# Delta-rule attention woven into a feed-forward layer: inverses by halves for every block, one block at a time, and Gram products on quarters of the array

## The chip, the core and the metric

The kernel runs on one core of one Trainium2 chip. The core's engines each run their own instructions in order: PE (TensorE, matmuls; PEld are its weight loads), DVE (VectorE), ACT (ScalarE), POOL (GpSimd) and SP (SyncE, which here only issues transfers). The metric is the device time of one execution in microseconds (us); the time shown for a kernel is the median of its runs. A profile is one execution recorded by the hardware profiler.

## The reference

Four sequences of 768 tokens, eight heads of 48 columns. First a recurrence over the tokens of each (sequence, head), then a feed-forward layer on what it gives, all in float32:

```python
k_n = k / (np.linalg.norm(k, axis=-1, keepdims=True) + 1e-06)
for t in range(S):                       # S = 768, state is 48 x 48 per (sequence, head)
    kt, vt, bt = (k_n[:, :, t], v[:, :, t], beta[:, :, t, None])
    y[:, :, t] = np.einsum('bhd,bhde->bhe', q[:, :, t], state)
    v_old = np.einsum('bhde,bhd->bhe', state, kt)
    state = state + bt[:, :, :, None] * np.einsum('bhd,bhe->bhde', kt, vt - v_old)

x = y.transpose(0, 2, 1, 3).reshape(B * S, H * D)       # 3072 x 384
h = x @ w_in                                            # w_in 384 x 2048
out = np.maximum(0.01 * h, h) @ w_out                   # w_out 2048 x 384
```

The two weight arrays arrive as float64.

## The kernel before

**Blocks.** The tokens are cut into chunks of 64. A block is the next chunk of all four sequences, so 256 tokens and 32 (sequence, head) pairs, in two groups of two sequences; there are twelve blocks. With G = K K^T of a chunk, n the norms and c = beta / n^2, a chunk needs T = (I + strict_lower(diag(c) G))^-1 diag(c) and A = strict_lower(Q K^T); then W = T n V - Kt S with Kt = T K, the next state S' = S + K^T W, and y = Q S + A W.

**Streams.** Five generators produce the work, each a few instructions per step:

- `weights`: 32 halves of weight rows. Each is converted from float64 words to an exact sum of two float32r parts: five or six DVE instructions of 384 columns (clamp L155, then L172, L173, L175, L176, or L160 to L166 for the nine in `FORMB`), ACT's absolute value and cast, POOL's sum and difference.
- `gram` (blocks in turn): for each sequence ACT writes K^T into a block-diagonal operand `kd` (`diag`, L109, two copies of 0.5 us), four matmuls of 96 rows, 128 by 128, give [G | A^T] of four pairs of heads in one PSUM tile (L279), ACT copies it to `gs` (L285), and a product with a triangle masks A^T (L286, on POOL; DVE in block 0 as L283 and block 1). G goes to DRAM (`gd`), A^T too (`ad`), and both are read back in other layouts: `gd` to the elimination's L and, for the blocks by halves, to `gm`; `ad` to the lower rows of the operand ring `rq`.
- `inv` (batches of blocks): T^T by elimination of columns on DVE. `eliminate` does for each column a product into `tmp` (L359 or L361) and a subtraction from T (L364), each often in two instructions for the even and odd rows. Blocks 0 and 1, each alone, and the pairs 2, 3 and 4, 5 go by halves: the two diagonal halves of 32 rows of each chunk are inverted on partitions of their own (31 columns), and the full T^T is put together later. The pairs 6, 7 and 8, 9 and 10, 11 go whole (`inv_whole`, 63 columns, 128 partitions). The results go to DRAM (`td`).
- `solve` (blocks in turn): loads the rings `rt` (T^T), `rv`, `rk`, `rq`; for blocks by halves `merge` multiplies the halves together on PE (`pz` L488, `pu` L496, with copies `zs` L490 on ACT and DVE between). Then `kt` (`pk` L558, and POOL's n V at L563), `step_w` (`pw` L571), `step_s` (`pc` L579), `step_y` (`py` L587), each 32 matmuls of a block and alternating between the two column halves of the array, and six transfers of y^T into `xl`, which is x^T of the block.
- `ffn` (blocks in turn): `xl` is split into `xh` and the rest (three pieces, ACT and DVE). For each of 16 slices f of the hidden layer nine matmuls of 256 columns give `ph` (L644); the relu is ACT's 0.01 h (L650) and DVE's maximum `t` (L651); ACT casts it to `gh` (L115), POOL takes the difference `gl` (L116); six matmuls of 384 columns add into `po` (L635), two slices later (`PD` = 2). `ph` has two buffers. At the end ACT copies `po` to `ob` (L666) and it is written.

**Order.** `weave` emits these streams side by side, at even paces set by a table of numbers at the end of the file; a scheduler then orders the instructions of each engine. Each engine runs its own list in order, so an instruction that waits holds up all behind it. `mark` and `behind` put some transfers behind a named instruction.

Of the kernel before, what the change touches and what calls it, by code (L numbers as in the profile page):

```python
# [30 lines left out]
HC = C // 2  # L31
P = 128
NCST = C + 64 + HS + 2 + 2
# [6 lines left out]
KQ_BUFS = 3  # L40
KT_BUFS, Q_BUFS = 2, 2
# [9 lines left out]
def delta_moe_kernel(ctx: ExitStack, tc, kqT, kv, qT, beta, cst, w_all, out, nblk):  # L51
    """A block holds the next chunk of each of the sequences.

    Recurrence of a chunk with G = K K^T, n = |k| + eps, c = beta / n^2:
      T = (I + strict_lower(diag(c) G))^-1 diag(c),  Kt = T K,  A = strict_lower(Q K^T)
      W = T n V - Kt S,  S' = S + K^T W,  y = Q S + A W
    """
# [7 lines left out]
    dr = ctx.enter_context(tc.tile_pool(name="dr", bufs=3, space=DRAM))  # L65
# [4 lines left out]
    NB = batches(nblk)  # L70
    where = {n: (b, i) for b, ns in enumerate(NB) for i, n in enumerate(ns)}
    Lh, gm = {}, {}

# [4 lines left out]
    eye0 = csb[:, C + 64:C + 64 + HS]    # of row (block, half, inverse), to column (inverse)  # L78
    blk = csb[0:HD, C + 64 + HS:C + 66 + HS]     # column h: row is of head h
    half = csb[:, C + 66 + HS:]  # L80
# [6 lines left out]

    def statics():
        for t in ring["t"]:
            nc.vector.memset(t, 0.0)  # L90
        for x in "vq":
            for t in ring[x]:
                nc.gpsimd.memset(t[0:R0], 0.0)

    def identities():
        with behind("rec"):
            for t in ring["k"]:
                nc.vector.tensor_copy(
                    t[0:R0].rearrange("p h u t -> p (h u) t"),
                    eye[:, 0:D].rearrange("p (o t) -> p o t", o=1).broadcast_to([R0, GH, D]))  # L100

    def dq(act):
        """The queue that a transfer is issued on"""
        return (nc.sync, nc.scalar)[act]

    def diag(dst, src, cols):
        """[row, pair, x] to [row, pair, h, x], 0 where the row is not of head h"""
        for h in range(2):
            nc.scalar.mul(dst[:, :, h], src, cols[:, h:h + 1])  # L109

# [1 line left out]
    wi, wo = ([{}, {}] for _ in range(2))  # L112
# [4 lines left out]

    def weights():
        """From float64 words to float32 (round to nearest; below float32's range to 0, above it to
        its largest), then to the two parts: sign, exponent and 20 bits of the fraction are taken  # L120
        from the high word, the low word counts 2^-52 of the exponent's power of two."""
        raws = {}

        def load(k):
            if k < 2 * NFC:
                raws[k] = raw = sb.tile([P, DO], U64, tag=f"w{k}", name=f"wr{k}", bufs=1)
                if k >= WAHEAD:     # not before the work on an earlier part, which this waits for
                    with behind("norms" if WGATE <= k < WGATE + 2 else "work"):
                        nc.vector.memset(raw[:, 0:1].bitcast(F32), 0.0)
                nc.sync.dma_start(raw, w_all[:, k // 2, k % 2])  # L130

        with behind("kq"):
            for k in range(WAHEAD):
                load(k)
        for k in range(2 * NFC):
# [5 lines left out]
            r = sb.tile([P, DO], F32, tag="cr", name=f"cr{k}", bufs=CB)  # L141
# [12 lines left out]
            with behind("rec" if RECA <= k < RECB else None):  # L154
                i = nc.vector.tensor_scalar(g, g, HI_MIN, HI_MAX, ALU.max, ALU.min)  # L155
            mark["work"] = i.ins
            load(k + WAHEAD)
            if k in FORMB:
                # the first part is cut off after 11 bits of the fraction, the second has the 23 bits behind them
# [11 lines left out]
            else:  # L171
                nc.vector.tensor_scalar(gi, gi, 3, 0x3FFFFFF8, ALU.logical_shift_left, ALU.bitwise_and)  # L172
                nc.vector.scalar_tensor_tensor(gi, hii, 0xC0000000, gi, ALU.bitwise_and, ALU.bitwise_or)  # L173
                if k in FORMD:
                    nc.vector.tensor_scalar(ri, gi, 0xFF800000, None, ALU.bitwise_and)  # L175
                    nc.vector.scalar_tensor_tensor(r, loi, 2.0 ** -52, r, ALU.mult, ALU.mult)  # L176
                else:
                    nc.scalar.mul(r, loi, 2.0 ** -52)
                    e = place("we", F32, DO)
                    nc.vector.tensor_scalar(e.bitcast(U32), gi, 0xFF800000, None, ALU.bitwise_and)  # L180
                    nc.gpsimd.tensor_tensor(r, r, e, ALU.mult)
# [5 lines left out]
    Gdr, Adr, Tdr, nrm, xls, mark = {}, {}, {}, {}, {}, {}  # L187

    def behind(name):
        """What is traced here is issued behind the marked instruction, on its engine."""  # L190
        return tc.issue_after(mark[name]) if name in mark else nullcontext()

    Lw, done = {}, set()

    def need(gen, fn, *blocks):
        for n in blocks:
            while (fn, n) not in done:
                next(gen)

    def by_halves(b):  # L200
        return b < NH

    def rows_of(b, i, e, g=None):
        """Partitions of a block's halves of inverses, (half, group, h, unit)"""
        a, w = i * 64 + e * HS, HS
        if g is not None:
            a, w = a + g * GH, GH
        return slice(a, a + w)

    def odd(b):  # L210
        """Whether a batch has the odd rows of T^T on partitions of their own, behind the even ones"""
        return by_halves(b) and len(NB[b]) == 1

# [26 lines left out]
    def gram(n):  # L240
# [9 lines left out]
        def load():  # L250
            if not ahead:
                return
# [555 lines left out]
```

## Time and profile before

| | us |
|---|---|
| median of 3 runs (lowest, highest) | 802.52 (793.92, 803.21) |
| span of the profiled execution | 800.6 |
| first FFN matmul | 113.5 |
| end of FFN block 0 (its copies of `ob`) | 202.65 |
| ends of blocks 1 to 5 | 269.76, 343.95, 411.40, 474.55, 530.83 |
| ends of blocks 6 to 11 | 568.36, 632.45, 673.28, 728.82, 762.78, 794.83 |

Two lines of the page's list of groups show how such a line is read: line of the code, engine, operation, output and input by the program's names, shape, count; then busy time and mean ns of one; then idle time of the engine just before them and what ended it.

```profile
L361 DVE SCALAR_TENSOR_TENSOR tmp<-T,cb,LA 128x252 f32<-128x252 f32 (+44 forms) x186 | 87.5, 503 | 2.2 <-POOL T L400 2.1
L109 ACT ACTIVATE kd<-kq,csb 96x256 f32<-96x256 f32 x94 | 42.1, 500 | 11.6 <-DMA kq<-in_kqT 10.9
```

A window's line has its start and end and its length, then for PE, PEld, DVE, ACT and POOL the busy time with the number of instructions, then the clock granted to PE as a share of full speed, the share of DMA time and GB/s. In a timeline a line is a start, a duration, the engine and the instruction with the count of equal neighbours; what stands in brackets is the idle time before it and what ended it. A matmul on float32 shows as two records. Times of matmuls are modelled at their ends, so a busy PE is not PE at its peak.

### The profile page before, as it was taken

Reading aid. Unit: us, or ns where it says so; the run is one execution under the profiler, and the core shown is the slowest. Engines: PE = TensorE matmul, PEld = TensorE weight load, DVE = VectorE, ACT = ScalarE, POOL = GpSimd, SP = SyncE. Lnnn points to the kernel's source line nnn. Section 1 sums busy time; section 2 is a strip of 40 time slices with the busy share of each in tenths; the row PEclk is TensorE's granted clock in tenths of the full one; section 3 lists DMA queues with packets and bytes.
Section 4 is the critical chain, followed back from the end, with each engine's and each line's share of the span. In section 5 each row is a group of like instructions: output and inputs, shape, how many; then the busy total and the mean of one; then the engine's idle time right before and its main releaser. Section 6 shows DMA issues by size and latency. Waiting matters only on the chain.

```text
span 800.6 us, 18926 instructions
## 1 busy us (share of the span) xinstructions
PE 648.8 (81%) x7000; PEld 600.8 (75%) x7000; DVE 602.9 (75%) x1684; ACT 380.1 (47%) x903; POOL 338.5 (42%) x371
## 2 busy tenths in 40 slices
PE   3343627786989897996998989989897999899997
PEld 3242516675989786986987978879786888899997
DVE  6988999999759308999994799996899997012221
ACT  5535543476547554553564353433634323545342
POOL 4327566755534433335336234344244343133332
PEclk9999957997997999897899999999999999999999
DMA  7987547532764596475325552312433102321000
GB/s 232 228 206 165 159 118 175 102 93 68 173 126 120 113 226 156 103 162 133 76 70 142 113 127 54 87 40 56 101 80 87 41 1 49 99 66 40 1 22 20
DMA packets 147547, 84.65 MB, mean 106 GB/s; under 512 B 114432, under 2 KB 126848, under 8 KB 147072
## 3 DMA queue, kind: packets, MB, share of 16 engines
q1 hardware_dynamic: 143120, 82.97, 43.8%
q8 instruction: 55, 0.90, 0.5%
q10 hardware_dynamic: 4336, 0.48, 0.5%
q14 instruction: 36, 0.29, 0.1%
HBM read 55.89 MB, written 22.81 MB: 98 GB/s over the span
## 4 chain that ended last, share of the span: by engine, by line
DVE 47%; PE 26%; DMA 14%; issue 5%; SPq 3%; ACT 2%; POOL 1%; DVEq 0%; ACTq 0%; POOLq 0%
DVE tmp L361 14%; DVE T L364 14%; PE ph L644 10%; PE po L635 10%; DVE t L651 4%; DVE tmp L359 3%; DMA td<-T 2%; PE pg L279 2%; DMA LA<-gd 2%; PE pk L558 2%; DMA rt<-td 2%; DVE cg L173 1%; DMA wr<-in_w_all 1%; DMA rq<-in_qT 1%; DVE cg L155 1%
## 5 line engine op out<-in xcount | busy, mean ns | idle before, releaser
L116 POOL TENSOR_TENSOR gl<-t,gh 128x256 fp32r<-128x256 f32 x192 | 163.9, 855 | 332.1 <-ACT gh L115 262.0
L644 PE MATMUL ph<-xh,w 128*128 128x256 f32 x1152 | 256.9, 300 | 42.4 <-DVE t L651 30.1
L644 PEld LDWEIGHTS ph<-xh,w 128*128 128x128 f32 x1152 | 200.7, 200 | 56.3 <-DVE t L651 40.4
L364 DVE TENSOR_TENSOR T<-T,tmp 128x120 f32<-128x120 f32 (+53 forms) x555 | 191.5, 375 | 0.9
L635 PE MATMUL po<-w,gh 128*128 128x384 f32 x768 | 187.4, 351 | 2.8 <-ACT gh L115 2.8
L115 ACT CAST gh<-t 128x256 fp32r<-128x256 f32 x192 | 77.6, 406 | 226.0 <-DVE t L651 191.1
L651 DVE TENSOR_TENSOR t<-ph,t 128x256 f32<-128x256 f32 x192 | 80.0, 418 | 136.1 <-ACT t L650 135.4
L644 PE MATMUL ph<-xl,w 128*128 128x256 f32 x576 | 169.2, 295 | 5.7 <-DVE xl L116 5.7
L635 PEld LDWEIGHTS po<-w,gh 128*128 128x128 f32 x768 | 135.2, 198 | 5.0 <-ACT gh L115 4.1
L644 PEld LDWEIGHTS ph<-xl,w 128*128 128x128 f32 x576 | 115.0, 200 | 7.7 <-DVE xl L116 7.2
L635 PE MATMUL po<-w,gl 128*128 128x384 f32 x384 | 116.2, 354 | 1.7 <-POOL gl L116 1.5
L650 ACT ACTIVATE t<-ph 128x256 f32<-128x256 f32 x192 | 72.5, 382 | 81.2 <-PE ph L644 69.5
L279 PE MATMUL pg<-kq,kd 96*128 96x128 f32 x376 | 68.0, 343 | 31.2 <-ACT kd L109 28.1
L361 DVE SCALAR_TENSOR_TENSOR tmp<-T,cb,LA 128x252 f32<-128x252 f32 (+44 forms) x186 | 87.5, 503 | 2.2 <-POOL T L400 2.1
L361 DVE SCALAR_TENSOR_TENSOR tmp<-T,cb,LB 128x220 f32<-128x220 f32 (+43 forms) x186 | 88.5, 504 | 0.1
L279 PEld LDWEIGHTS pg<-kq,kd 96*128 96x128 f32 x376 | 61.3, 247 | 35.2 <-ACT kd L109 30.5
L635 PEld LDWEIGHTS po<-w,gl 128*128 128x128 f32 x384 | 71.1, 196 | 4.7 <-POOL gl L116 3.6
L359 DVE TENSOR_TENSOR tmp<-T,Lh 128x28 f32<-128x28 f32 (+42 forms) x183 | 59.2, 347 | 0.7
L286 POOL TENSOR_TENSOR gs<-gs,csb 128x256 f32<-128x256 f32 x40 | 35.9, 901 | 33.9 <-ACT gs L285 28.6
L563 POOL TENSOR_TENSOR rv<-rv,nt 64x384 f32<-64x384 f32 x48 | 43.4, 934 | 15.1 <-issue 13.4
L109 ACT ACTIVATE kd<-kq,csb 96x256 f32<-96x256 f32 x94 | 42.1, 500 | 11.6 <-DMA kq<-in_kqT 10.9
L183 POOL TENSOR_TENSOR cg<-cg,cr 128x384 f32<-128x384 f32 x23 | 27.9, 1218 | 30.9 <-DVE cr L176 30.9
(89 smaller groups left out, 718.9 us busy)
## 6 DMA issues: line engine op xcount, KB each, us to landing
wr<-in_w_all SPq DMA_DIRECT2D x32, 384.0 KB, 4.0
kq<-in_kqT SPq DMA_DIRECT2D x47, 192.0 KB, 3.8
gd<-gs SPq DMA_DIRECT2D x48, 128.0 KB, 3.1
ad<-gs SPq DMA_DIRECT2D x24, 256.0 KB, 3.2
rq<-ad SPq DMA_DIRECT2D x24, 256.0 KB, 4.8
rv<-in_kv SPq DMA_DIRECT2D x24, 192.0 KB, 4.6
rk<-in_kv SPq DMA_DIRECT2D x24, 192.0 KB, 4.0
rq<-in_qT SPq DMA_DIRECT2D x24, 192.0 KB, 4.2
```

Of the source, the lines that this page charges most:

```text
L109: nc.scalar.mul(dst[:, :, h], src, cols[:, h:h + 1])
L115: nc.scalar.copy(hi, src)
L116: lo_eng.tensor_tensor(lo, src, hi.bitcast(F32), ALU.subtract)
L279: nc.tensor.matmul(pv[:, :, p], kd[:, p].rearrange("p h t -> p (h t)"), kq[:, p], start=True, stop=True)
L359: nc.vector.tensor_tensor(tv, a, l, ALU.mult)
L361: nc.vector.scalar_tensor_tensor(tv, a, c[:, j:j + 1], l, ALU.mult, ALU.mult)
L364: i = nc.vector.tensor_tensor(t, t, tv, ALU.subtract)
L563: nc.gpsimd.tensor_tensor(v[DN, :, us], v[DN, :, us], nt[DN, g, :, us].rearrange("p h (u o) -> p h u o", o=1).broadcast_to([C, 2, NPAIR, D ...
L635: nc.tensor.matmul(po[t][:, :DO], a[:, ts_], w[f], start=(f == 0 and k == 0), stop=(f == NFC - 1 and k == 2))
L644: nc.tensor.matmul(ph[:, :TB], a[f][:, cc * P:(cc + 1) * P], x[:, cc], start=(k == 0), stop=(k == 3 * NCC - 1))
L650: nc.scalar.mul(t, ph[:, :TB], 0.01)
L651: nc.vector.tensor_tensor(t, ph[:, :TB], t, ALU.max)
```

## The change

- Every block's inverse goes by halves, one block at a time: 16 rows on 128 partitions, 31 columns, even and odd rows in two instructions each (60 products at L269 and 60 subtractions at L274 per block). `inv_whole` is gone, `merge` runs for all blocks (`pz` L325, `pu` L333).
- Gram: `kd` is gone. K^T and Q^T of the two parities of heads lie on partitions 0 to 47 and 64 to 111; 32 matmuls of a block (L202, 48 rows, 64 by 128) each take a quarter of the array: row half b, column half c, head c ^ b. Two PSUM tiles per group.
- The results go straight into operands: A^T is masked on DVE from PSUM into the ring `rq` (L217, four of 64x256 per group), the lower left of G is copied by POOL into `gm` (L221). Only the diagonal halves of G go through DRAM, in eight transfers (L210), and come back contiguous (L226). `ad` and the read of `gm` from DRAM are gone. The inverse goes to DRAM as `td` (L299) and `tt` (L301).
- The queue of those transfers is ACT's for blocks 0 and 1, SP's for the others (`dq`).
- The order is written out: FFN of block n with `solve` of n + 1, the inverse of n + 2, `gram` of n + 3. Weights: eight beside the first inverse, eight beside the second, the rest beside the first FFN block; `rq` has four buffers instead of two, `cr` two instead of three.

```diff
-def batches(nblk):
-    return [[0], [1]] + [[n, n + 1] for n in range(2, nblk, 2)]
+    def dq(n):
+        return nc.scalar if n < 2 else nc.sync
...
     def gram(n):
-            kd = sb.tile([P, NPAIR, 2, C], F32, tag="yt", name=f"kd{n}_{q}", bufs=YT_BUFS)[0:HD]
-            diag(kd, kq[:, :, 0], blk)
             for p in range(NPAIR):
-                nc.tensor.matmul(pv[:, :, p], kd[:, p].rearrange("p h t -> p (h t)"), kq[:, p], start=True, stop=True)
-                nc.scalar.copy(gs[:, :, us], pv)
-                (nc.vector if n == 0 else nc.gpsimd).tensor_tensor(gs[:, 1, us], gs[:, 1, us], trib, ALU.mult)
-                        nc.sync.dma_start(gd[g, h].rearrange("u j i -> j u i"), gs[h * C:(h + 1) * C, 0])
-                    nc.sync.dma_start(ad[g], gs[:, 1])
+                for c in range(2):
+                    for b in range(2):
+                        r = slice(b * R0, b * R0 + D)
+                        nc.tensor.matmul(ps[b][c * 64:(c + 1) * 64, p * 128:(p + 1) * 128],
+                                         kq[r, c ^ b, p, 0], kq[r, c ^ b, p].rearrange("p x t -> p (x t)"),
+                                         start=True, stop=True)
+            for b in range(2):
+                nc.scalar.copy(gs[:, b], pv[b][:, 0])
+                    dq(n).dma_start(
+                        gd[a:a + GU].rearrange("l j i -> j l i"),
+                        gs[c * 64 + e * HC:c * 64 + (e + 1) * HC].rearrange("p b u t -> p (b u) t")[:, :, e * HC:(e + 1) * HC])
+                    nc.vector.tensor_tensor(
+                        qa[DN, c, b * NPAIR:(b + 1) * NPAIR], pv[b][r, 1],
+                        tri[r].rearrange("p (o t) -> p o t", o=1).broadcast_to([C, NPAIR, C]), ALU.mult)
+                nc.gpsimd.tensor_copy(m[R0 + HC:P, c].rearrange("p (b u) t -> p b u t", b=2),
+                                      gs[c * 64 + HC:(c + 1) * 64, :, :, 0:HC])
...
     def inv(n):
+        for j in range(HC - 1):
+            eliminate(n, L, j, T, j // 2 + 1)
+                nc.vector.tensor_copy(Tt.rearrange("p i m -> p m i"), T)
+                        dq(n).dma_start(td[e].rearrange("(m x) l i -> x l m i", x=2)[er], T[a:a + HS])
+                    dq(n).dma_start(tt.rearrange("l i (x m) -> x l i m", x=2)[er], Tt[er * 64:er * 64 + HS])
...
     def merge(n, g, t):
-            nc.sync.dma_start(t[R0 + e * HC:R0 + (e + 1) * HC].rearrange("p h u i -> p (h u) i")[:, :, e * HC:(e + 1) * HC],
-                              td[0, :, rows_of(b, i, e, g)])
+            dq(n).dma_start(t[R0 + e * HC:R0 + (e + 1) * HC].rearrange("p h u i -> p (h u) i")[:, :, e * HC:(e + 1) * HC],
+                            T[e, :, gl])
+        dq(n).dma_start(gt[0:HC], Tt[gl].rearrange("l i m -> i l m"))
...
-    weave(nblk * NF,
-          (gg, G2, 0, GB), (gg, G, GB, LEADG),
-          (iv, inv_steps(2), IV0, I2), (iv, sum(inv_steps(b) for b in range(3, len(NB))), I2, I2 + (nblk - 4) * LEADI),
-          (sv, m * NS, 0, m * LEADS),
-          (wg, 2 * NFC, 0, WE), (chain(ffn, range(nblk)), nblk * NF, 0, nblk * NF))
+    weave(32, (iv, NI, 0, 32), (gg, NGR, 0, 8), (wg, W0, 0, 32))
+    identities()
+    weave(32, (sv, NS, 0, 24), (iv, NI, 0, 32), (wg, W1, 0, 32), (gg, NGR, 26, 32))
+    for n in range(nblk):
+        weave(NF, (ff, NF, 0, NF), (wg, 2 * NFC, 0, 12),
+              (sv, NS if n + 1 < nblk else 0, 0, 12), (iv, NI if n + 2 < nblk else 0, 0, NF), (gg, NGR if n + 3 < nblk else 0, 8, NF))
...
-WG, WS, WE, W0, W1, RECA, RECB = 5, 0, 12, 6, 6, 0, 32
+W0, W1 = 8, 8
```

What the scheduler made of it shows in each engine's list. First DVE, where the first split of x (`xl`, the last thing before the first FFN matmul can go) stands. Before, ahead of it are 20 clamps (L155), and it lies amid the columns of the second inverse and a weight:

```order
L155 TENSOR_SCALAR cg_1323<-cg_1323 128x384
L129 MEMSET wr_1327 128x2
L364 TENSOR_TENSOR T_787<-T_787,tmp_19_0_975 128x2x5x12
L172 TENSOR_SCALAR cg_1323<-cg_1323 128x384
L359 TENSOR_TENSOR tmp_20_0_994<-T_787,Lh_210 128x132
L116 TENSOR_TENSOR xl_696<-xl_696,xh_1289 128x256
L173 SCALAR_TENSOR_TENSOR cg_1323<-wr_1071,cg_1323 128x384
L364 TENSOR_TENSOR T_787<-T_787,tmp_20_0_994 128x2x6x11
L116 TENSOR_TENSOR xl_696<-xl_696,xh_1289 128x256
```

After, ahead of it are all 32 clamps (now L144), the whole second inverse and the masks of the next gram:

```order
L269 TENSOR_TENSOR tmp_30_0_1183<-T_607,L_323 128x8
L274 TENSOR_TENSOR T_607<-T_607,tmp_30_0_1183 128x8
L293 COPY Tt_608<-T_607 128x16x32
L217 TENSOR_TENSOR rq_75<-pg_0_0_1135,csb 64x256 x2
L217 TENSOR_TENSOR rq_75<-pg_0_1_1136,csb 64x256 x2
L217 TENSOR_TENSOR rq_76<-pg_1_0_1215,csb 64x256 x2
L111 TENSOR_TENSOR xl_658<-xl_658,xh_1248 128x256
L217 TENSOR_TENSOR rq_76<-pg_1_1_1216,csb 64x256 x2
L111 TENSOR_TENSOR xl_658<-xl_658,xh_1248 128x256 x2
```

So the twelve weights that stood behind the first split of x now stand ahead of it, as does the end of the second inverse.

Second, ACT at the same place. Before, the casts of x are followed by the first activation at once:

```order
L519 COPY nt_1399<-pn_1397 64x32
L115 CAST xh_1289<-xl_696 128x256
L115 CAST w_1270<-cg_1259 128x384
L115 CAST xh_1289<-xl_696 128x256
L115 CAST w_1285<-cg_1274 128x384
L115 CAST xh_1289<-xl_696 128x256
L650 ACTIVATE t_0_1308<-ph_0_1298 128x256
```

After, the transfers of the second inverse (`td`, `tt` out, `rt`, `gm` in) are issued between, on the same engine:

```order
L206 COPY gs_1_1213<-pg_1_1_1216 128x256
L110 CAST xh_1248<-xl_658 128x256 x2
L350 COPY nt_1465<-pn_1463 64x32
L312 DMA rt_79<-td_1190 32x16x32 x2
L314 DMA gm_0_218<-tt_1191 32x16x32
L312 DMA rt_80<-td_1190 32x16x32 x2
L320 COPY gm_0_218<-gm_0_218 32x16x2x16
L314 DMA gm_1_292<-tt_1191 32x16x32
L465 ACTIVATE t_0_1267<-ph_0_1257 128x256
```

The first activation of FFN block 0 now stands behind a read of `td`, which waits for its write, and behind a copy of what was read.

Third, PE in the FFN. Before, a gram of one sequence is four matmuls in a row, between the products of the FFN:

```order
L496 MATMUL pu_1_3310<-zs_1_3291,gm_1_3285 32x32 x16
L279 MATMUL pg_1_3366<-kq_1_3205,kd_1_3367 128x128 x4
L279 MATMUL pg_2_3380<-kq_2_3207,kd_2_3381 128x128 x4
L644 MATMUL ph_2_3651<-xh_3542,w_254 128x256
```

After, a group is sixteen matmuls whose PSUM tiles alternate; the second group of a block is cut up by `ph` and `po`:

```order
L451 MATMUL po_1_1256<-w_1621,gl_12_2180 128x384
L202 MATMUL pg_1_0_2390<-kq_1_2206 64x128
L202 MATMUL pg_1_1_2391<-kq_1_2206 64x128
L202 MATMUL pg_1_0_2390<-kq_1_2206 64x128
L202 MATMUL pg_1_1_2391<-kq_1_2206 64x128
L460 MATMUL ph_15_2312<-xh_1248,w_1760 128x256
```

The number of places behind the first `ph` where PE's list goes from products of the FFN to others or back is 181 before and 291 after.

More of the change, by code (lines that the diff above doesn't have):

```diff
@@ L32 @@
 P = 128
[L33 removed]
+NCST = C + 64 + HS + 2
 EPS = 1e-6
@@ L95, in identities, with behind @@
     def identities():
[L96 to L109, printed above, removed]
+        for t in ring["k"]:
+            nc.vector.tensor_copy(
+                t[0:R0].rearrange("p h u t -> p (h u) t"),
+                eye[:, 0:D].rearrange("p (o t) -> p o t", o=1).broadcast_to([R0, GH, D]))
     wi, wo = ([{}, {}] for _ in range(2))
+    raws, mark = {}, {}
+    def behind(name):
+        return tc.issue_after(mark[name]) if name in mark else nullcontext()
     def split(src, hi, lo, lo_eng):
@@ L116, in split, with load_w @@
         lo_eng.tensor_tensor(lo, src, hi.bitcast(F32), ALU.subtract)
-    def weights():
[L122 to L134, printed above, removed]
+    def load_w(k):
+        if k < 2 * NFC:
+            raws[k] = raw = sb.tile([P, DO], U64, tag=f"w{k}", name=f"wr{k}", bufs=1)
+            if "work" in mark:
+                with behind("work"):
+                    nc.vector.memset(raw[:, 0:1].bitcast(F32), 0.0)
+            nc.sync.dma_start(raw, w_all[:, k // 2, k % 2])
+    def weights():
         for k in range(2 * NFC):
@@ L185, in weights @@
             yield
[L187 to L208, printed above, removed]
@@ L457, in inv_halves @@
+                Tts[n] = td, tt
+                done.add((inv, n))
             yield
[L459 to L463 removed]
     def merge(n, g, t):
[L467 to L477 removed]
+        T, Tt = Tts[n]
```

492 lines of the change are left out of this document (150 added, 342 removed).

## The prediction

> **What bounds the kernel now.** I read the page's busy shares first, then its 40 slices, then windows cut at the first FFN product and at the copies of `ob` that end each FFN block, then the waits of PE.
>
> ```profile
> PE 648.8 (81%) x7000; PEld 600.8 (75%) x7000; DVE 602.9 (75%) x1684; ACT 380.1 (47%) x903; POOL 338.5 (42%) x371
> ...
> PE   3343627786989897996998989989897999899997
> ...
> DVE  6988999999759308999994799996899997012221
> ```
>
> ```profile
> 0.00:113.50 113.50, 45.15 (x452) 40.50 (x452) 97.61 (x331) 57.37 (x125) 54.03 (x53) 0.93 0.75 187
> 113.50:202.65 89.15, 64.76 (x673) 57.50 (x674) 87.73 (x185) 47.41 (x111) 56.68 (x57) 0.84 0.49 116
> 202.65:794.83 592.18, 538.72 (x5877) 502.84 (x5875) 417.53 (x1172) 274.43 (x667) 227.77 (x263) 0.95 0.39 89
> 794.83:800.60 5.77, 0.14 (x1) 0.00 (x0) 0.00 (x0) 0.86 (x2) 0.00 (x0) 0.80 0.28 68
> ...
> 343.95:411.40 67.45, 58.45 (x724) 54.14 (x723) 66.11 (x160) 31.17 (x75) 26.61 (x27) 0.90 0.45 101
> 568.40:632.45 64.05, 55.95 (x710) 51.18 (x710) 62.02 (x147) 28.56 (x67) 25.00 (x25) 0.96 0.33 80
> 673.28:728.82 55.54, 52.49 (x691) 49.48 (x692) 8.42 (x21) 29.80 (x68) 14.91 (x20) 0.97 0.33 82
> 762.78:794.83 32.05, 31.69 (x222) 31.52 (x222) 6.61 (x16) 12.55 (x33) 11.79 (x16) 1.00 0.06 14
> ```
>
> Each window has its length, then busy time of PE, PEld, DVE, ACT and POOL, and the granted clock. The bound differs by stage. Up to 113.5 us and through the first FFN block to 202.65 DVE is it: 185 of those 202.7 us (weights and inverses). The eleven blocks behind are PE's (539 of 592), except where a whole inverse fills DVE (66.1 of 67.5, 62.0 of 64.1), and there PE waits for `t`. The last row is an FFN block alone: 32.0 us of PE at full clock.
>
> ```profile
> PE ph L644 <- DVE t L651: 22.9, 21, 3.1
> PE ph L644 <- ACT xh L115: 8.0, 3, 3.6
> PE pg L279 <- ACT kd L109: 7.5, 4, 3.3
> PE pu L496 <- DVE zs L490: 3.5, 4, 1.2
> ```
>
> These are PE's waits between 202.65 and 794.83 (total, times, longest). The profiled span is 800.6, 1.9 below the median 802.5; I sum against the span and add 1.9.
>
> **The change, part 1: the start.** Before, 20 of 32 weight conversions stand on DVE ahead of the first split of x; after, all 32, with both inverses complete and 22 masks. Prices of one conversion, from DVE's groups between 56.5 and 122 us, and of a mask read from PSUM:
>
> ```profile
> L173 DVE SCALAR_TENSOR_TENSOR cg<-wr,cg 128x384 uint32<-128x384 uint32 x13 | 9.7, 753 | 0.0
> L176 DVE SCALAR_TENSOR_TENSOR cr<-wr,cr 128x384 f32<-128x384 uint32 x12 | 6.5, 550 | 0.0
> L155 DVE TENSOR_SCALAR cg<-cg 128x384 f32<-128x384 f32 x15 | 6.3, 428 | 3.5 <-ACT cg L153 3.5
> L172 DVE TENSOR_SCALAR cg<-cg 128x384 uint32<-128x384 uint32 x13 | 6.1, 479 | 0.1
> L175 DVE TENSOR_SCALAR cr<-cg 128x384 uint32<-128x384 uint32 x13 | 5.9, 461 | 0.1
> ...
> L283 DVE TENSOR_TENSOR gs<-pg,csb 128x256 f32<-128x256 f32 x4 | 1.7, 420 | 0.7 <-ACT gs L282 0.7
> ```
>
> One weight is 0.75 + 0.55 + 0.43 + 0.48 + 0.46 = 2.7 us, so twelve more are 33 us. Masks go from 8 to 22: 14 x 0.42 = 6. The eliminations on DVE before that point were 159 records of 45 us:
>
> ```profile
> L359 DVE TENSOR_TENSOR tmp<-T,Lh 128x60 f32<-128x60 f32 (+32 forms) x80 | 22.8, 310 | 0.1
> L364 DVE TENSOR_TENSOR T<-T,tmp 128x60 f32<-128x60 f32 (+32 forms) x79 | 22.2, 306 | 0.0
> ```
>
> Now they are 240 instructions. Their pace, where nothing disturbs them, is in the timeline of the first inverse (start, time; two instructions to a line), and the two windows show POOL's part in it:
>
> ```profile
> 31.41 0.96 DVE L359 TENSOR_TENSOR tmp<-T,Lh 128x31 f32<-128x31 f32 x2
> ...
> 43.58 0.35 DVE L359 TENSOR_TENSOR tmp<-T,Lh 128x64 f32<-128x64 f32 x2
> 43.84 0.35 DVE L364 TENSOR_TENSOR T<-T,tmp 128x64 f32<-128x64 f32 x2
> ```
>
> ```profile
> 31.40:34.80 3.40, 2.15 (x11) 1.86 (x9) 3.40 (x8) 1.00 (x3) 3.32 (x4) 1.00 1.05 224
> 34.80:37.90 3.10, 1.47 (x7) 1.47 (x8) 3.10 (x24) 0.00 (x0) 0.05 (x1) 1.00 1.06 219
> ```
>
> The last two lines start 0.26 us apart, so 0.13 us an instruction; but while POOL runs four products (3.32 us), DVE gets through 8 instead of 24: each POOL operation costs DVE (3.40 - 8 x 0.13) / 4 = 0.6 us. So 240 x 0.13 = 31 to some 50 us against 45: -14 to +5, and I take 0. First FFN product: 113.5 + 33 + 6 = 153 (140 to 165).
>
> **Part 2: the first FFN block** loses the 12 weights that filled DVE (12 x 2.7 = 33 of its 87.7 us) and costs what a steady block costs (part 3, 56.5), with two extras. The loads of its merge (`td`, `tt`, `rt`, `gm`) are now on ACT's queue ahead of `t_0`'s activation, and the load waits for the inverse's write. The nearest row is the same path in the first inverse, done at 56.2:
>
> ```profile
> 56.23 0.11 DVE L364 TENSOR_TENSOR T<-T,tmp 128x8 f32<-128x8 f32 x1
> ...
> 68.10 1.92 PE L488 MATMUL pz<-rt,gm 32*32 32x32 f32 x64 [16.45 <-DMA rt<-td]
> ```
>
> That is 11.9 us; some 5 us of it pass in the copy, masks and splits of x on DVE that stand between. I take 7 (0, if the load lands early, to 12). The clock was 0.84 to 0.92 there: 0.9 of 47 warm us costs 3 us more than the 2 of a steady block. Hence 56.5 + 7 + 1 = 64.5 against 89.15, its end at 217 (205 to 232) against 202.65: the start as a whole loses 14 us.
>
> **Part 3: blocks 1 to 8.** PE's work at full clock: FFN 32.0; solve `pk`, `pw`, `pc`, `py`, from runs of them (64, 62, 30 and 31 records of the 64 each has): 2.0 + 2.1 + 1.8 + 2.2, with `pn` 8.3; merge, now in every block instead of the first four, `pz` and `pu` of a group 0.69 each: 4 x 0.7 and the zs copies' gap, 3.0.
>
> ```profile
> 284.49 1.99 PE L558 MATMUL pk<-rt,rk 64*48 64x64 f32 x64
> 691.33 2.06 PE L571 MATMUL pw<-rv,rt 128*64 128x48 f32 x62
> 255.02 0.88 PE L579 MATMUL pc<-rv,rk 128*48 128x48 f32 x30
> 255.75 1.08 PE L587 MATMUL py<-rq,rv 128*48 128x64 f32 x31
> 225.88 0.69 PE L488 MATMUL pz<-rt,gm 32*32 32x32 f32 x32 [0.40 <-DMA rt<-td]
> 329.21 0.69 PE L496 MATMUL pu<-zs,gm 32*32 32x32 f32 x30
> 209.38 1.05 PE L279 MATMUL pg<-kq,kd 96*128 96x128 f32 x8
> 237.48 2.90 PE L279 MATMUL pg<-kq,kd 96*128 96x128 f32 x16
> ```
>
> Gram before: four sequences at 1.05, 4.2 us a block, 0.26 a product. After, 32 products of 128 columns on quarters. No row shows four quarters. Not overlapping, 32 x 0.26 = 8.4. By pairs, from `pk` (32 products of 64 columns on two column halves, 62 ns each): 32 x 0.125 = 4.0. All four at once: 2.1. I take 3.3, between pairs and quarters, since quarters differ from `pk` only in the rows. The rule beside it: the Trainium skill, "TensorE: Matmul & The Clock Gate", section Part 3 (Packing small matmuls), says that tiles at different rows and columns run at once, for some 4 ns more each; by it the gram is 2.1 and the sum 12 us lower. No run here shows it yet.
>
> So 32 + 8.3 + 3.0 + 3.3 = 46.6 us warm. On top of it:
>
> - DVE late. An inverse is 120 instructions on DVE every block, between `t_5` and `t_12`: 120 x 0.13 = 16, 7 relus x 0.42 = 3, `Tt` and copies 1, and about 10 POOL operations x 0.6 = 6: 26 us. PE has there 7 f x 2.0, `pw`, `pc`, `py` (6) = 20, and one f in hand: 22. Late by 4.
> - The boundary of two blocks (three splits of x): 8.0 us of waits for xh in 11 blocks and about as much again at the clock's cost, 1.3. The zs copy: up to 1.2 a block, now in all.
> - Clock, 0.96 of 47: 2.0.
> - Switches between FFN and small products: each side of one costs little over 0.13 (0.29 + 0.15 below stand 0.5 apart, where a `po` alone takes 0.34), and there are 110 more: 14 us in 11 blocks, 1.3.
>
> ```profile
> 252.41 0.29 PE L579 MATMUL pc<-rv,rk 128*48 128x48 f32 x2
> 252.62 0.44 PE L635 MATMUL po<-w,gh 128*128 128x384 f32 x1
> ```
>
> A block: 46.6 + 4 + 1.3 + 1.2 + 2.0 + 1.3 = 56.4. Check by before's row without DVE work: 55.5 (673.28).
>
> What the rest costs. Masks of A^T move from POOL to DVE: 8 x 0.42 = 3.4 us a block at its end (`t_12` on), where no elimination is left; hidden, and if not, 3 us on `t_13`. POOL loses four masks and gains four `gm` copies: nothing. kd's ACT copies (8 x 0.5 a block) go, and with them a 7.5 us wait in all; the new copies of two PSUM tiles replace the old ones. Two transfers through DRAM go; rows of `td` and `tt` get shorter, on queues whose DMA share is 0.39: hidden, since an inverse is asked for a block later.
>
> **Sum.** 217 to the end of block 0; eight blocks x 56.4 = 451; block 9, without a gram, 53; block 10, without inverse and `pc`, 45.5; block 11, 32; tail 6: 804.5, and 1.9: 806.5. So no change that can be told: about 2% (16 us) is what a measurement here separates. The start loses 14, the eleven blocks win 10.
>
> **Rivals.**
> - Faster: DVE keeps up and PE is the bound. For it: POOL and DVE are seen to take turns, and where DVE's stream is dense POOL is the one that waits; then no 4 us, the gram nearer 2.1: 51.5 a block, 209 + 412 + 49 + 44 + 32 + 6 = 752, 760 with half a lag. Against it: 22.9 us of waits for `t` before, with POOL no busier.
> - Slower: DVE's eliminations in the FFN go at 0.2 us each, the first inverse's mean (24.8 us from 31.4 to 56.2 for 120, with masks among them) instead of 0.13 and POOL's six. That is 24 + 4 + 6 = 34 against 22: 12 late in ten blocks, +80 at the far end, 846 with half. It decides from 0.14: +1.2 us a block for each 0.01.
> - Slower: the quarters don't overlap (8.4): nine grams x 5.1 = 46, 852. Against it: `pk`, halves at once.
> - Slower: the price of switches. The array is drained at each. At 0.13 it is in the sum; it would take 0.4 to matter (110 x 0.27 = 30 us, 836). The Trainium skill, "TensorEngine Tiling (Array Packing)", section Key Properties, says that changing the tiling mode drains the TensorE, which speaks against this change with its 291 changes for 181; the 252.62 row agrees that there is a price, 0.1 us.
>
> **Chances.** My forecast (787 to 818) 0.40; the faster rival 0.30; slower 0.30, of which DVE's pace 0.15, quarters 0.05, switches 0.05 and a start later than 230 us 0.05. The range reaches from the faster rival's middle to the slower one's: 760 to 848. Faster by over 2% 0.30, within 2% 0.40, slower 0.30.
>
> **What would show it.** First FFN product at 153 and `ob` of block 0 near 217, else part 1 or 2 is off. `ob` copies then 56 apart: 51 means the faster rival. PE's waits for `t` of about 4 us a block; `pg` records of 32 products taking 3.3; a DVE busy near 50 us a block in blocks 1 to 8. If the first product is on time and the blocks too, but the tail isn't, the sum was right by chance.

## The result

The changed kernel took 849.48 us (median of 4 runs, 847.2 to 851.17) against 801.09 for the kernel before (median of 4): ratio 1.0615, 95% interval 1.0563 to 1.0668. It is slower by 6%. I had forecast 806.5 with a range of 760 to 848, so the measured time lies just above the range.

The page of the changed kernel, its busy shares and the slices of PE, DVE and the granted clock:

```profile
PE 641.8 (76%) x8152; PEld 583.2 (69%) x8152; DVE 546.0 (64%) x2205; ACT 356.0 (42%) x867; POOL 293.6 (35%) x379
...
PE   4100001579989989899799799798897997989997
...
DVE  7689999949429629459378296394593772951121
...
PEclk9999999968989989979989899999999998999999
```

PE has next to nothing to do in slices 2 to 7 (21 to 149 us), while DVE is nearly full. Behind that DVE goes up and down once in each block, and PE has a dip to 7 or 8 once in each. The windows, cut as before at the first FFN product and at the copies of `ob` (the row from 422.21 at the second copy of each end, 1.2 to 1.5 us behind the first):

```profile
0.00:179.37 179.37, 32.72 (x516) 29.37 (x516) 156.36 (x498) 54.70 (x119) 83.88 (x87) 0.98 0.52 122
179.37:244.94 65.57, 60.00 (x703) 54.43 (x704) 40.77 (x175) 28.58 (x70) 20.07 (x29) 0.84 0.36 66
...
422.21:479.76 57.55, 52.51 (x690) 47.28 (x690) 37.55 (x167) 26.56 (x66) 18.44 (x26) 0.94 0.38 77
...
763.19:810.36 47.17, 45.09 (x557) 42.84 (x558) 9.15 (x21) 22.05 (x52) 11.48 (x16) 0.96 0.14 30
810.36:843.85 33.49, 32.42 (x227) 32.05 (x225) 6.70 (x16) 13.22 (x34) 11.76 (x16) 1.00 0.05 13
```

| stage | before | forecast | measured |
|---|---|---|---|
| first FFN product | 113.5 | 153 | 179.4 |
| end of FFN block 0 | 202.65 | 217 | 244.9 |
| blocks 1 to 8, each | | 56.4 | 58.2 |
| blocks 9, 10, 11 | | 53, 45.5, 32 | 52.4, 47.2, 33.5 |
| blocks 1 to 11 together | 592.2 | 581.5 | 598.9 |
| span | 800.6 | 804.5 | 849.4 |

So 42 of the 49 us that the change costs are lost up to the end of FFN block 0, and 7 in the eleven blocks behind it. Against the forecast 28 of 45 us are in the start, 15 in blocks 1 to 8.

**The start.** DVE's groups up to the first FFN product (busy time, mean ns, idle time before), and the end of the first inverse in the timeline:

```profile
L269 DVE TENSOR_TENSOR tmp<-T,L 128x60 f32<-128x60 f32 (+24 forms) x120 | 34.0, 312 | 0.1
L274 DVE TENSOR_TENSOR T<-T,tmp 128x60 f32<-128x60 f32 (+24 forms) x120 | 30.8, 285 | 0.2
...
L217 DVE TENSOR_TENSOR rq<-pg,csb 64x256 f32<-64x256 f32 x21 | 8.9, 422 | 10.8 <-ACT gs L206 10.4
...
L238 DVE TENSOR_SCALAR sr<-L 128x32 uint32<-128x32 uint32 x2 | 0.4, 188 | 5.2 <-DMA L<-gd 5.2
```

```profile
131.91 0.59 DVE L293 COPY Tt<-T 128x512 f32<-128x512 f32 x1
```

The first inverse ends at 132 us; before, its last column ended at 56. The eliminations take 64.8 us against 45.0 (the sums of the two groups), and DVE waits for ACT (10.4) and for L (5.2). Two lines of POOL and four of DVE, from their timelines at the same place, show why a column is dear there:

```profile
106.61 1.03 POOL L111 TENSOR_TENSOR w<-cg,w 128x384 fp32r<-128x384 f32 x1 [0.62 <-ACT w L110]
109.08 1.17 POOL L166 TENSOR_TENSOR cg<-cg,cr 128x384 f32<-128x384 f32 x1 [1.43 <-DVE cr L164]
```

```profile
106.72 1.00 DVE L269 TENSOR_TENSOR tmp<-T,L 128x54 f32<-128x54 f32 x1
...
108.32 0.20 DVE L274 TENSOR_TENSOR T<-T,tmp 128x54 f32<-128x54 f32 x1
...
108.92 0.21 DVE L269 TENSOR_TENSOR tmp<-T,L 128x60 f32<-128x60 f32 x1
...
109.32 0.99 DVE L269 TENSOR_TENSOR tmp<-T,L 128x48 f32<-128x48 f32 x1
```

The same product takes 0.2 us, or 1.0 while a POOL operation on a weight runs.

**The blocks.** PE's waits in blocks 1 to 8 (total, times, longest):

```profile
PE ph L460 <- DVE t L466: 22.0, 11, 3.6
PE po L451 <- POOL gl L111: 16.5, 7, 2.9
```

All but three short ones (0.3 to 0.6 us) of the waits for `t` fall into the first fifth of a block, most at its very beginning. The timelines around one boundary, that of 479.8, in order of time (SPq is SP issuing transfers):

```profile
459.20 0.68 SPq L418 DMA_DIRECT2D xl<-yt  x1
...
460.40 0.61 DVE L293 COPY Tt<-T 128x512 f32<-128x512 f32 x1
...
467.33 0.59 SPq L420 DMA_DIRECT2D xl<-yt  x1
468.01 2.00 SPq L210 DMA_DIRECT2D gd<-gs  x4
470.12 2.02 SPq L299 DMA_DIRECT2D td<-T  x4
472.24 1.29 SPq L301 DMA_DIRECT2D tt<-Tt  x2
473.72 0.52 POOL L280 MEMSET T<- 128x512 f32 x1 [5.07 <-DMA td<-T]
474.20 0.72 POOL L111 TENSOR_TENSOR gl<-t,gh 128x256 fp32r<-128x256 f32 x1
475.61 0.30 SPq L314 DMA_DIRECT2D gm<-tt  x1
477.94 0.64 ACT L320 COPY gm<-gm 32x512 f32<-32x512 f32 x1 [5.72 <-DMA gm<-tt]
480.14 0.67 ACT L465 ACTIVATE t<-ph 128x256 f32<-128x256 f32 x2
481.04 0.58 PE L460 MATMUL ph<-xh,w 128*128 128x256 f32 x1 [3.10 <-DVE t L466]
481.42 0.42 PE L460 MATMUL ph<-xl,w 128*128 128x256 f32 x1
481.64 0.63 PE L460 MATMUL ph<-xh,w 128*128 128x256 f32 x2
```

The inverse is done at 461.0, but its write is issued at 470.1: SP issues the twelve transfers of y and four of `gd` first, one behind the other, most at 0.5 to 0.7 us each. The read into `gm` lands at 477.9, ACT has waited 5.7 us for it, and the first activation of the new block stands behind the copy. PE idles 3.1 us, and then a product of 256 columns starts every 0.21 us instead of every 0.12, for some 7 us: the clock in such a stretch is 0.64.

```profile
422.00:431.50 9.50, 8.02 (x94) 7.30 (x94) 2.50 (x7) 4.32 (x13) 4.62 (x6) 0.64 0.82 181
```

### The profile page after: what moved, and what is told of

It is laid out like the page before. It is cut to its first block, busy times and chain, and to the rows that moved or that the text cites. A ratio compares the mean times of both kernels' runs of the same rounds, so it can differ in the third digit from the quotient of the medians.

```text
span 849.4 us, 21690 instructions
## 1 busy us (share of the span) xinstructions
PE 641.8 (76%) x8152; PEld 583.2 (69%) x8152; DVE 546.0 (64%) x2205; ACT 356.0 (42%) x867; POOL 293.6 (35%) x379
## 4 chain that ended last, share of the span: by engine, by line
PE 43%; DVE 20%; DMA 17%; SPq 7%; ACT 6%; issue 5%; POOL 1%; ACTq 1%; DVEq 0%; POOLq 0%
PE ph L460 17%; PE po L451 15%; DVE tmp L269 4%; DVE T L274 4%; DMA L<-gd 3%; DMA tt<-Tt 3%; DMA gm<-tt 2%; DMA wr<-in_w_all 2%; PE pk L373 2%; DMA kq<-in_kqT 2%; PE py L405 2%; PE pw L386 2%; DVE t L466 2%; SPq L299 2%; SPq L210 2%
## 5 line engine op out<-in xcount | busy, mean ns | idle before, releaser
L460 PE MATMUL ph<-xh,w 128*128 128x256 f32 x1152 | 266.6, 309 | 34.7 <-DVE t L466 26.3
L111 POOL TENSOR_TENSOR gl<-t,gh 128x256 fp32r<-128x256 f32 x192 | 142.4, 744 | 360.4 <-ACT gh L110 314.2
L460 PEld LDWEIGHTS ph<-xh,w 128*128 128x128 f32 x1152 | 206.6, 206 | 47.2 <-DVE t L466 30.2
L269 DVE TENSOR_TENSOR tmp<-T,L 128x31 f32<-128x31 f32 (+9 forms) x720 | 154.7, 252 | 0.5
L274 DVE TENSOR_TENSOR T<-T,tmp 128x31 f32<-128x31 f32 (+9 forms) x720 | 144.6, 235 | 0.9
L451 PE MATMUL po<-w,gl 128*128 128x384 f32 x384 | 123.6, 349 | 16.5 <-POOL gl L111 16.5
L325 PE MATMUL pz<-rt,gm 32*32 32x32 f32 x768 | 22.0, 203 | 98.5 <-DMA rt<-td 98.5
L325 PEld LDWEIGHTS pz<-rt,gm 32*32 32x32 f32 x768 | 17.7, 116 | 100.1 <-issue 99.2
L217 DVE TENSOR_TENSOR rq<-pg,csb 64x256 f32<-64x256 f32 x96 | 40.6, 423 | 35.0 <-ACT gs L206 33.8
L202 PE MATMUL pg<-kq 48*64 48x128 f32 x768 | 46.2, 310 | 16.1 <-DMA kq<-in_kqT 8.6
L202 PEld LDWEIGHTS pg<-kq 48*64 48x64 f32 x768 | 32.2, 150 | 29.9 <-issue 12.8
L320 ACT COPY gm<-gm 32x512 f32<-32x512 f32 x24 | 15.1, 639 | 64.4 <-DMA gm<-tt 64.2
```

What stands on the lines that cost most here:

```text
L111: lo_eng.tensor_tensor(lo, src, hi.bitcast(F32), ALU.subtract)
L202: nc.tensor.matmul(ps[b][c * 64:(c + 1) * 64, p * 128:(p + 1) * 128], kq[r, c ^ b, p, 0], kq[r, c ^ b, p].rearrange("p x t -> p (x t)"), s ...
L217: nc.vector.tensor_tensor(qa[DN, c, b * NPAIR:(b + 1) * NPAIR], pv[b][r, 1], tri[r].rearrange("p (o t) -> p o t", o=1).broadcast_to([C, NP ...
L269: nc.vector.tensor_tensor(tv, t[:, :, j:j + 1].broadcast_to([P, k, w]), L[:, j, j + 1:].rearrange("p (o w) -> p o w", o=1).broadcast_to([P ...
L274: nc.vector.tensor_tensor(t, t, tv, ALU.subtract)
L325: nc.tensor.matmul(zv[h * 64:h * 64 + HC, u], gt[lo, l], t[lo, h, u, HC:], start=True, stop=True)
```

## The experiments

Times are medians; the kernel before ran beside each group, and ratios are against it. The groups (e1 to e4, e5 to e8, e9 to e11, e12) ran on four chips, where the kernel before took 798.2, 801.3, 799.7 and 802.5 us, so a few us between runs of different groups tell nothing. Times of stages are those of one profiled execution of each kernel.

**e1, the weights gated.**

```diff
+            with behind("rec"):
                 i = nc.vector.tensor_scalar(g, g, HI_MIN, HI_MAX, ALU.max, ALU.min)
...
+        if n == 0:
+            mark["rec"] = i.ins
```

> The changed kernel with one thing put back: each weight's clamp on DVE is held behind the last column of block 0's inverse that has been written out so far, as before the change. Theory (the start lost its 28 us of extra delay because weights and masks stand amid the first inverse, which ends at 132 us instead of 56, and PE has nothing to do until then): the first inverse ends near 70, the first FFN product comes at 115 to 135 instead of 179, and although the FFN's first block then carries weights, it ends near 215 instead of 245; total about 820. Rival (what sets the start is DVE's total work, 91 us of weights and 65 of eliminations slowed by POOL, in whatever order): the first block still ends at 240 to 245 and the total stays at 845 to 850.

834.78 us, ratio 1.0475 (1.0425 to 1.0525). The first FFN product came at 123.7, as the theory had it, but the first block ended at 229.6, halfway between the two. The order costs 15 us; the rest is DVE's work, which the gate only moves into FFN block 0 (now 106 us instead of 66).

**e2, the gm copy later.**

```diff
+        mark["hi"] = nc.scalar.copy(hi, src).ins
...
+        with behind("gh"):
             nc.scalar.copy(gt[r1].rearrange("p l (m e) -> p l e m", e=2), ...)
...
+            mark["gh"] = mark["hi"]
```

> The changed kernel with ACT's copy that reorders gm (two per block) held behind the cast of the first FFN slice of the block, so that it no longer stands ahead of the first activation. Theory (at each block's boundary ACT waits some 5.7 us for the read of tt, the FFN's first relu stands behind it, PE idles 3 us and then runs some 7 us at half clock): a steady block goes from 58 to 52 us, PE's waits for t (22 us in blocks 1 to 8) nearly vanish, total 849 to about 800. Rival (DVE is late with the relus amid the eliminations, as predicted, 4 us a block): blocks stay at 57 to 58, total within 5 us of 849. Second rival (only the wait moves: the merge comes later and PE waits for rt instead): blocks 56, total 835.

848.85 us, 1.063 (1.0588 to 1.0672): nothing. FFN block 0 became 10 us shorter (55.8) and ended 14 us earlier, but the blocks behind it gave that back: blocks 1 to 8 became 0.6 us longer each (58.8), block 9 four. PE's waits from 231 to 701 us show where the wait went:

```profile
PE po L452 <- POOL gl L111: 18.6, 12, 3.1
PE ph L461 <- DVE t L467: 12.5, 9, 5.6
PE pk L374 <- DVE rt L338: 5.1, 7, 0.9
PE pk L374 <- ACT rt L340: 3.3, 5, 0.7
```

Some is gone from `t` and turns up at `gl` and in front of `pk`. My theory that ACT's copy is the cause fell; it is where the lateness shows.

**e3, the memset later.**

```diff
-        nc.gpsimd.memset(T, 0.0)
+        with behind("gl"):
+            nc.gpsimd.memset(T, 0.0)
...
+            mark["gl"] = mark["lo"]
```

> The changed kernel with POOL's memset of T held behind the last slice's gl, so that gl of the last slice no longer waits for the write of td. Theory (the 16.5 us that PE waits for gl in blocks 1 to 8 are 2 us a block on their own): total down by 10 to 16 us, to 835. Rival (the first relu of the next block is held by ACT until the same time, so that this wait costs nothing as long as that one is there): total within 4 us of 849, with PE's waits for t up by what those for gl go down.

847.47 us, 1.0615 (1.0578 to 1.0651). The time stays, as the rival had it, but not by its way. PE's waits for `gl` (16.5 us) vanish, and those for `t` go only from 26.3 to 29.6 over the whole run. What comes in their place in blocks 1 to 8 is a wait of the merge's products for the read of `td`, 2.1 us before:

```profile
PE pz L326 <- DMA rt<-td: 19.4, 8, 3.0
```

So the memset, too, was only the place where a late `td` showed.

**e4, all three.**

> The three edits together. If the three causes are separate and add: start -28, blocks -6 x 9, gl -2 x 8: 850 - 95 = 755, below the kernel before (801). If the start is DVE's total work: 780. If the blocks are held by DVE's relus: 815.

834.55 us, 1.0465 (1.0422 to 1.0509): what e1 alone gives. Blocks stayed at 57.8, and PE again waited at `pz` for the read of `td` itself (14.9 us in blocks 1 to 8). Whatever is moved out of the way, the merge waits for `td`; what stands ahead of its write is SP's row of issues quoted above.

**e5, the inverse written from ACT's queue.**

```diff
-                        dq(n).dma_start(td[e]...)
+                        nc.scalar.dma_start(td[e]...)
-                    dq(n).dma_start(tt...)
+                    nc.scalar.dma_start(tt...)
```

> The changed kernel with the write of the inverse (td and tt, six transfers a block) issued by ACT in every block instead of by SP from block 2 on. In the trace of the changed kernel the inverse is done at 461.0 and td is issued at 470.1, behind sixteen other issues of SP at 0.5 to 0.7 us each. Theory (SP's row of issues makes the merge late; ACT's copy of gm, the first relu, PE's 3 us of idle time, its half clock and POOL's memset all hang on it): gm lands before the boundary, a block goes from 58 to 51 to 53, total 849 to 795 to 810. Rival (the round trip through DRAM is what is too long, whoever issues it, or ACT is held up by its six issues of 0.5 us): blocks 57 to 59, total 840 to 855.

817.77 us, 1.0201 (1.0141 to 1.0262): 32 us less than the changed kernel, of which 25 in blocks 1 to 8, now 55.0 on the mean (58.4 in e6, which ran beside it). The timelines of the same place (ACTq is ACT issuing) and the window of that block:

```profile
448.30 1.28 ACTq L301 DMA_DIRECT2D tt<-Tt  x2
...
449.81 0.53 POOL L280 MEMSET T<- 128x512 f32 x1 [0.32 <-DMA td<-T]
...
455.82 0.49 SPq L314 DMA_DIRECT2D gm<-tt  x1
...
458.34 0.65 ACT L320 COPY gm<-gm 32x512 f32<-32x512 f32 x1 [1.09 <-DMA gm<-tt]
```

```profile
405.92:460.52 54.60, 50.94 (x690) 46.53 (x690) 36.98 (x167) 26.53 (x67) 20.90 (x30) 0.97 0.41 82
```

The inverse is on its way 12 us before the boundary, ACT's wait for `gm` falls from 5.7 to 1.1, the memset's from 5.1 to 0.3, and the clock rises from 0.94 to 0.97. The gain is two thirds of what I expected. PE's only waits from 245 to 680 us are now for `t`, and they have grown:

```profile
PE ph L460 <- DVE t L466: 32.9, 25, 3.6
```

In blocks 1 to 8, 33.1 us of waits stand against 41.8 of all kinds in the changed kernel; 12 of them lie at the boundaries (0.2 to 2.2 us each) and 21 inside the blocks, where the changed kernel had 3. So 16 of the 25 us are not waits: PE's busy time falls from 422.8 to 406.8 us, at a clock of 0.98 instead of 0.95. The read is still issued by SP, behind y and `gd`; that this keeps the waits at the boundary is likely, but no run shows it, and none parts the causes of those inside.

**e6, the start's transfers on SP.**

```diff
-        return nc.scalar if n < 2 else nc.sync
+        return nc.sync
```

> The changed kernel with the transfers of blocks 0 and 1 (gd, L, td, tt, rt, gm) issued by SP instead of ACT. My prediction put 7 us of FFN block 0 on ACT being held by them. If that holds: first FFN product within 5 us of 179, first block's end 7 us earlier, total about 842. If ACT's issues also hold back gs, and with it the masks and L at the start (DVE waits 10 and 5 us for these): the first product 10 us earlier too, total about 832. Rival (SP is late as well, with twelve issues for xl and the weights' loads in front): total 849 or more.

834.48 us, 1.0423 (1.0366 to 1.048). The first FFN product came at 159.7 and the first block ended at 229.1, 16 us earlier. DVE's groups of the start lost their waits:

```profile
L217 DVE TENSOR_TENSOR rq<-pg,csb 64x256 f32<-64x256 f32 x16 | 6.8, 423 | 0.4
...
L238 DVE TENSOR_SCALAR sr<-L 128x32 uint32<-128x32 uint32 x2 | 1.0, 498 | 0.2 <-DMA L<-gd 0.2
```

DVE's idle time ahead of the first product fell from 23.0 to 6.7 us: ACT's issues had held back its own copies to `gs`, and with them the masks and L. FFN block 0 itself is not shorter (69.3 against 65.6): part of the gain goes back there.

**e7, e8, e9, e10: the edits together.** e7 is e1 and e5; e8 adds the memset and `q = (nc.sync, nc.scalar)[h]` for y in all blocks; e9 is e1, e6 and e5 from block 2 on; e10 is e9 with the memset.

> Weights gated by the first inverse (as in e1) and td and tt on ACT's queue (as in e5). If the start and the boundaries are two separate losses, the gains add: -16 for the start and what e5 brings for the blocks; by the theory of SP's queue 849 - 16 - 45 = 788, below the kernel before (798 to 803). If e5 brings nothing: 835.

810.19 us, 1.0121 (1.0066 to 1.0175). Start and boundaries are separate losses, nearly additive: 39 us against 15 + 32.

> As e7, and with half of the transfers of y (six of twelve a block) on ACT's queue, and POOL's memset of T behind the last slice's gl. By the theory of SP's queue the boundary has nothing left to wait for: blocks 50 to 52, total 770 to 785. If ACT, with 12 issues of 0.5 us a block, is now what is late: blocks 56 or more, 830.

828.87 us, 1.0344 (1.0278 to 1.0409): worse than e7, blocks at 58. ACT then issues twelve transfers a block, but the scheduler also put the merge of the next block two slices earlier, so this run doesn't tell which of the two costs the time.

> Three queue edits at once: weights gated by the first inverse (e1), the transfers of blocks 0 and 1 on SP (e6), td and tt on ACT from block 2 on (e5). Theory (three separate losses: the order at the start, ACT's issues at the start, SP's row at the boundaries): first FFN product 110 to 115, first block's end 213 to 218, blocks 54, total 790 to 798, level with the kernel before or up to 2% below. Rival (in the start DVE's work is the bound as soon as its order is right, so that e1 and e6 win the same 15 us): first block's end 228, total 806 to 812 as e7.

805.43 us, 1.007 (1.0039 to 1.0101). The first product came at 115.9, the first block ended at 221.6, between theory (213 to 218) and rival (228). The total lies beside the rival's 806 to 812 and not within the theory's 790 to 798; blocks 1 and 2 took 60, the others 55.

> As e9, and POOL's memset of T behind the last slice's gl. By e3 the memset alone brought nothing that can be told, since the first relu was held until the same time; with td early that cover is gone, but so is most of what the memset waits for: within 4 us of e9. If it still costs 1 to 2 us a block: 8 to 12 us below e9.

802.4 us, 1.0041 (1.0013 to 1.0068): 3 us below e9, inside what was expected of it, and no difference that the intervals separate.

**e11, the weights' second part from ACT.**

```diff
-                split(g, d0, d1, nc.gpsimd)
+                nc.scalar.copy(d0, g)
+                nc.scalar.copy(d1, g)
```

> The changed kernel, where the second part of 23 of the 32 weights is not worked out: ACT copies the weight a second time in place of POOL's difference, so 23 POOL operations of 1.06 us in the start become 23 of 0.5 us on ACT, and DVE's own list is the same. In the trace of the changed kernel eliminations take 1.0 us instead of 0.2 while POOL works. Theory (POOL's operations hold up DVE 0.6 to 0.8 us each): eliminations and weights of the start 15 us shorter, first FFN product at 160 to 165 instead of 179, total 830 to 836. Rival (DVE's instructions are slow there for another reason, or POOL's remaining products fill the gaps): first product at 175 or later, total 845 or more.

This kernel leaves out the second part of 23 weights, so its output is not the layer's; it serves to time the start. 831.89 us, 1.0396 (1.0355 to 1.0437); the first product came at 159.7, 19.7 us earlier, for 23 POOL operations less: 0.86 us each, of which 17.5 us in all are DVE's busy time (156.4 to 138.8). The same two groups of DVE up to there:

```profile
L270 DVE TENSOR_TENSOR tmp<-T,L 128x60 f32<-128x60 f32 (+24 forms) x120 | 28.8, 268 | 0.2
L275 DVE TENSOR_TENSOR T<-T,tmp 128x60 f32<-128x60 f32 (+24 forms) x120 | 26.2, 247 | 0.2
```

They fall from 64.8 to 55.0 us with the list of DVE unchanged. So POOL's work does slow DVE, and half of the 20 us by which the eliminations had grown over before came from these 23 operations alone.

**e12, all weights in the form with one POOL operation**, on top of e10:

```diff
-FORMB = [0, 1, 2, 3, 4, 5, 12, 24, 26]
+FORMB = list(range(32))
```

> As e10, and all 32 weights in the form that nine have (six DVE instructions instead of five, one POOL operation instead of two, four ACT instructions instead of two). By e11 a POOL operation in the start costs DVE 0.87 us (20 us for 23), a sixth DVE instruction 0.35: 23 x (0.87 - 0.35) = 12 us less on DVE up to the end of the first FFN block: 211 to about 199, total 802 to 790, 1% below the kernel before. Rival (POOL's operations that are left, or ACT's 46 more copies of 0.5 us, take what is gained): 800 to 806.

793.56 us, 0.9891 (0.9865 to 0.9917): 1.1% below the kernel before, clear of 1 by the interval but under the 2% that I took as what can be told. It is 9 us below e10, where 12 were expected; the first block ends at 202.7, where the kernel before has it. Whether the change's structure is worth something is not shown by this: the kernel before has the same 23 weights in the form with two POOL operations, and it was not run with all 32 in the other form.

## Why the prediction was wrong

**First FFN product, 153 forecast, 179 measured: terms mis-sized.** This is the larger part of the miss, 26 us. The weights cost 40 us instead of 33 (91.0 us for 32, against 51.2 ahead of that point before), the masks 5 instead of 6. The eliminations, "-14 to +5, and I take 0", cost 20 more than before. I had measured that a POOL operation costs DVE 0.6 us, and then priced the start's columns by the range of before's, though twelve more weights bring one or two POOL operations each into the stretch; e11 puts the price at 0.86. And DVE idles 7 us more, for ACT's issues: e6 wins 20 us at the first product by that one line. I had counted these issues only once, at FFN block 0. e1 shows the third part, the order: 56 us at the first product, 15 at the end of the block. At the end of block 0 e1, e6 and e11 win 15, 16 and 20 us; e1 and e6 together (e9) win 23 and not 31, so parts of these are the same. The busy times of groups overlap, so the terms add to more than the 66 us between 113.5 and 179.4.

**FFN block 0, 64.5 forecast, 65.6 measured: right in number, by luck.** I had put 7 us on the first activations, held by the transfers on ACT's queue. PE doesn't wait for `t` once in this block. The stall behind ACT's copy of `gm` comes at its end, with the inverse of block 2, whose transfers are on SP's queue:

```profile
238.34 0.63 ACT L320 COPY gm<-gm 32x512 f32<-32x512 f32 x1 [7.07 <-DMA gm<-tt]
239.73 0.58 PE L460 MATMUL ph<-xh,w 128*128 128x256 f32 x1 [3.35 <-ACT xh L110]
```

The casts of x stand behind that copy, and the read of `gm` stood behind the same sixteen issues of SP (it goes out at 236.0). With the copies later (e2) the block takes 55.8 us, of which 6 of the 10 us won are PE's busy time, at a clock of 0.92 instead of 0.84. With the transfers off ACT's queue (e6) it takes 69.3, so the queue that I had priced is not what fills it.

**Blocks 1 to 8, 56.4 forecast, 58.2 measured: near in sum, wrong in its parts.** PE is busy for 52.8 of the 58.2 and waits for 5.2. The FFN was undersized: I read 32.0 from before's last block, whose first two slices of `ph` lie ahead of its window (222 records in it, where the FFN's 16 slices of 15 products have 240). A slice takes 2.12 us in the last block at full clock, two products of the same place in two slices:

```profile
826.95 0.28 PE L460 MATMUL ph<-xh,w 128*128 128x256 f32 x1
...
829.07 0.28 PE L460 MATMUL ph<-xh,w 128*128 128x256 f32 x1
```

Sixteen are 33.9, and before's block 10, an FFN with nothing beside it, took 34.0 (728.82 to 762.78). The gram was oversized: a group of sixteen products took

```profile
460.51 1.10 PE L202 MATMUL pg<-kq 48*64 48x128 f32 x32
```

so all four quarters ran at once, 2.1 to 2.2 us a block instead of 3.3. The rule of the Trainium skill ("TensorE: Matmul & The Clock Gate", Part 3) agrees with this row, and I should have taken its end of the range (over nine grams it is 11 us, and not the 12 that I wrote). "DVE late by 4" hardly exists: three waits of 0.3 to 0.6 us inside eight blocks. The stretch that I had put at 26 us takes 21.3 from the first elimination to the last (0.16 us each, with seven POOL operations beside them and not ten), just under the 22 that I gave PE.

In its place stood what I had costed at nothing, the way of the inverse through DRAM: "rows of `td` and `tt` get shorter, on queues whose DMA share is 0.39: hidden, since an inverse is asked for a block later". This is the step that failed in the blocks: waits for `t`, `gl` and `td` that hang on this way are 38 of PE's 42 us of waits in blocks 1 to 8, 4.7 us a block, and the clock is 0.95. I looked at how busy the DMA engines are, not at SP, which issues some 50 transfers a block one after the other, and I took the next block's work for work a block away. The inverse ends at 461, the products of its merge stand behind the second slice of the next block, 16 us on, and 9 of these pass before SP comes to its write. e5 wins 32 us by mending the write alone.

**The rivals.** The time came out on the slower side, but by none of the mechanisms that I had priced for the blocks: the eliminations go at 0.16 us and not 0.2, quarters overlap, and the switches cost 0.1 us a side (a `ph` behind other products starts its successor after 0.22 instead of 0.12). What did come, POOL against DVE and a start later than 230 us, I had at 0.05 for the start. The faster rival's 51.5 a block was reached by no run; the nearest is e5 with 55.0, its merge still late.

**Against before.** Blocks 1 to 9 together are 8 us shorter than before (518 against 526): the two long blocks with whole inverses (67.4 and 64.1 us) are gone, but every block now has its stall at the boundary. Block 10 is 13 us longer (47.2 against 34.0), because before it was an FFN alone and now has the `solve` of block 11 beside it, as I had forecast (45.5). So the eleven blocks take 599 against 592. In the start the change costs 42.

## What to carry to other kernels

Count the transfers that each queue has to issue in a stretch, and what stands ahead of the one that is waited for: at 0.5 to 0.7 us an issue a row of sixteen delays a result by 9 us while the DMA engines look idle. When work moves between engines that hold each other up, price it in the company that it will have, not by its pace alone. And where a wait is found, follow it back to the transfer or instruction that is late; e2 and e3 moved the place of the wait and won nothing, e4 won no more than its part e1, and e5 moved the cause.

## What the runs showed of the hardware

A POOL operation of 1.0 to 1.2 us held up DVE's float32 products by 0.8 us each (0.2 to 1.0 us), and 23 of them less brought 20 us. PE's clock fell to half with pauses of 1.9 us (for `gl`, until 475) and 3.1 us (for `t`, until 481), 6 us apart, and stayed there for some 7 us. The Trainium skill ("TensorE: Matmul & The Clock Gate", Part 1) gives an idle window of some 3.4 us for it; the pauses here were each shorter. It need not be two of them: in e5 one pause of 2.0 us (until 353.2) was followed by a clock of 0.64 over 4.8 us, and one of 1.8 us (until 639.0) by full clock over 5.9. What decides between such pauses these runs don't tell.
